# Cosine attention and token/channel mixer on one core: rows of a head laid out as three chunks of 128 and one of 64 instead of four of 112

## The chip, the cores and the metric

The kernel runs on one core of a Trainium2 chip. The metric is the device time of one execution in microseconds (us). Each version is executed several times; the median counts. Beside the times there is one profiled execution of the kernel, whose trace gives the durations used below.

## What is computed

The inputs are q, k and v with 8 batches, 12 heads, 448 rows and 64 features, in float32, and four weight matrices. The reference, cut to what matters:

```python
q_n = q / (norm(q, axis=-1) + 1e-06)
k_n = k / (norm(k, axis=-1) + 1e-06)
scores = q_n @ k_n.T / tau                  # per batch and head, 448 x 448
attn = softmax(scores)
x = (attn @ v), heads side by side          # 8 x 448 x 768
h = relu(x.T @ w_tok1) @ w_tok2             # 448 -> 256 -> 448, along the rows
u = x + h.T
out = u + relu(u @ w_ch1) @ w_ch2           # 768 -> 1536 -> 768, along the features
```

Row order inside a batch is free within the kernel, as long as q's rows, the output rows and the two token weights agree on it. Both versions use this freedom: they read several neighbouring rows of a head into one partition, and write the output rows back to where they belong.

## The kernel before

**Attention.** Two heads make a pair; there are 48 pairs, six per batch. `load` (line 151) brings q, k and v of a pair with one DMA each on the queue of SyncE (SP): partition p gets rows 4p to 4p+3 of a head, a run of 1 KB, so that a head lies as four chunks of 112 rows on 112 partitions. `squares` (line 164) squares q and k on GpSimd, `norm_sum` (177) adds up over the 64 features on VectorE, `norm_root` (181, 182) takes the root on ScalarE as exp(0.5 ln), `norm_rec` adds epsilon (186) and takes the reciprocal (188) on VectorE, and `normalize` (196) multiplies on GpSimd, four instructions of 256 elements per partition. The two heads are then transposed together to 128 features by 448 rows, in the first eleven pairs on TensorE (`tpose_pe`, 222, with a copy out of PSUM, 227 or 229), later by a DMA transpose on SP (`tpose_dma`, 213). `score` (241) computes the transposed scores: for each of four chunks of keys, two matmuls, one for each head. Head 0 uses rows 0 to 63 of the array, head 1 rows 64 to 127. `expo` (248) takes the exponential of a chunk, both heads in one ScalarE instruction of 896 elements per partition. `pv` (262) multiplies with v, which has a column of ones for the sum of the softmax: for each of four blocks of 128 query rows, 2 heads x 4 chunks = 8 matmuls with 65 columns; blocks 0 to 2 are the first half (24 matmuls), block 3 the second (8). Lines 268 and 269 divide.

**Mixer.** For each batch, `tok1` (293) and `tok2` (306, and 311 for the rows that two batches share in one tile) apply the token weights; the sum u goes to float32 and float16, and its float16 form is transposed by DMAs on SP (319 for batch 0, 327 later) into uT. `ch1` (335) needs all of uT of the batch; `ch2` (344) and the addition (348) follow, then `store` (363). A batch has three tiles of 128 rows, its odd neighbour four, the fourth of which holds the last 64 rows of both.

**Order of the work.** The order on every engine is written out by hand and kept by the program. For pairs 0 to 9 (`opening`) the mixer has little or nothing to give to TensorE; from pair 10 (`slot`) the mixer of the batch before is cut into jobs, and `fill` puts some of them between the attention steps, by costs and a credit per slot. Loads run four pairs ahead: `load(i + 4)` stands at the head of slot i in SP's queue, and after it there come, in this order of issue, the DMA transposes of uT, the transposes of normalized q and k of pair i + 2, and the stores. SP works through its queue in order, so an entry that waits holds up all behind it. Weights come with casting DMAs on GpSimd's queue (131, 136) and with plain ones on SP (110, 113, 114, 119); ScalarE casts the token weights to float16 in slots 3 to 5 (122, 125), w2 with a change of its column order.

**The tile of the array.** A matmul names a tile of TensorE's array. In the built program `pv`, `ch1`, `ch2`, `tok1` and most of `tok2` use the full 128 x 128, `score` uses 64 x 128 (64 rows, 128 columns) at rows 0 and 64, and line 311 uses 128 x 64 at columns 0 and 64.

## Time and profile before

| | |
|---|---|
| median of 3 runs | 417.53 us (416.78 to 418.73) |
| profiled execution | 414.94 us, of which its span is 413.2 us and 1.7 us lie around it |
| granted TensorE clock, mean | 0.991 |
| busy, share of the span | TensorE 94%, ScalarE 64%, VectorE 54%, GpSimd 53% |
| first ch1 matmul | at 62.5 us |
| last score matmul | at 351.6 us; then soon only the mixer of the last batch |
| DMA | 64.31 MB in 100249 packets, 96816 of them from the queues of SP and ScalarE |

"Span" is from the first to the last instruction; positions in the text are microseconds from its start. PE is TensorE's matmul row and PEld its weight loads, DVE is VectorE, ACT ScalarE, POOL GpSimd, SP (SPq) SyncE's queue. A row of a group of instructions names the line, the engine, the operation and the tiles (out<-in) with shapes as partitions x elements, a count, the busy time and the mean duration of one. Matmuls overlap in the pipeline, so that their mean duration is longer than their distance from start to start; where a matmul's cost matters, the distance is used.

### The profile page before, as it was taken

Reading aid. Unit: us, or ns where it says so; the run is one execution under the profiler, and the core shown is the slowest. Engines: PE = TensorE matmul, PEld = TensorE weight load, DVE = VectorE, ACT = ScalarE, POOL = GpSimd, SP = SyncE. Lnnn points to the kernel's source line nnn. Section 1 sums busy time; section 2 is a strip of 40 time slices with the busy share of each in tenths; the row PEclk is TensorE's granted clock in tenths of the full one; section 3 lists DMA queues with packets and bytes.
Section 4 is the critical chain, followed back from the end, with each engine's and each line's share of the span. In section 5 each row is a group of like instructions: output and inputs, shape, how many; then the busy total and the mean of one; then the engine's idle time right before and its main releaser. Section 6 shows DMA issues by size and latency. Waiting matters only on the chain.

```text
span 413.2 us, 8942 instructions
## 1 busy us (share of the span) xinstructions
PE 386.9 (94%) x3512; PEld 219.8 (53%) x3512; DVE 222.8 (54%) x520; ACT 263.0 (64%) x457; POOL 217.6 (53%) x307
## 2 busy tenths in 40 slices
PE   1787759999999999999999999999999999999996
PEld 1454535555545556555545556555545556655453
DVE  4786966649634575438643575448643573152022
ACT  5879767975587566766578566766578565521410
POOL 5999968856675465636675465636674440000000
PEclk9998998999999999999999999999999999999999
DMA  7999899876984478736865488738976453015013
GB/s 228 229 269 245 161 171 256 147 203 144 216 191 124 123 189 224 179 90 157 218 176 145 115 173 229 176 90 122 226 208 157 79 120 98 2 40 152 2 38 114
DMA packets 100249, 64.31 MB, mean 156 GB/s; under 512 B 60400, under 2 KB 96752, under 8 KB 100208
## 3 DMA queue, kind: packets, MB, share of 16 engines
q1 hardware_dynamic: 96816, 58.89, 58.2%
q0 software_dynamic: 3264, 4.72, 7.3%
q8 instruction: 27, 0.44, 0.4%
q10 hardware_dynamic: 128, 0.15, 0.1%
q14 instruction: 14, 0.11, 0.1%
HBM read 43.45 MB, written 11.01 MB: 132 GB/s over the span
## 4 chain that ended last, share of the span: by engine, by line
PE 82%; DVE 9%; ACT 5%; DMA 2%; issue 1%; POOL 0%; POOLq 0%; ACTq 0%
PE pG L335 27%; PE pF L344 26%; PE pO L262 10%; PE pS L241 10%; PE pR L293 5%; PE pU L306 3%; DVE u L316 3%; ACT pE L248 2%; DVE ssq L177 2%; DMA uT<-u 2%; DVE x L269 1%; DVE nre L186 1%; PE pU L311 1%; DVE u L324 1%; DMA ql<-in_q_dram 1%
## 5 line engine op out<-in xcount | busy, mean ns | idle before, releaser
L248 ACT ACTIVATE pE<-pS 112x896 f16<-112x896 f32 x192 | 165.7, 913 | 40.2 <-PE pS L241 39.3
L335 PE MATMUL pG<-uT,wc1t 128*128 128x384 f16 (+1 forms) x576 | 121.7, 354 | 0.2 <-DMA uT<-u 0.2
L196 POOL TENSOR_TENSOR qkn<-ql,rn 112x256 f16<-112x256 f32 x96 | 58.4, 627 | 112.6 <-DVE rn L188 103.1
L344 PE MATMUL pF<-wc2t,gT 128*128 128x384 f16 x672 | 116.4, 326 | 0.0
L344 PEld LDWEIGHTS <-gT 128*128 128x128 f16 x672 | 63.6, 98 | 47.1 <-issue 7.4
L337 ACT ACTIVATE gT<-pG 128x384 f16<-128x384 f32 (+1 forms) x96 | 52.6, 548 | 47.3 <-PE pG L335 46.6
L335 PEld LDWEIGHTS <-wc1t 128*128 128x128 f16 x576 | 51.2, 98 | 51.7 <-issue 11.8
L241 PE MATMUL pS<-qkT 64*112 64x448 f16 x384 | 63.0, 393 | 13.2 <-ACT pE L248 7.2
L348 DVE TENSOR_TENSOR u<-pF,u 128x384 f32<-128x384 f32 x56 | 31.1, 556 | 80.7 <-PE pF L344 80.7
L262 PEld LDWEIGHTS <-pE 112*128 112x128 f16 x1536 | 62.9, 100 | 18.0 <-issue 6.8
L262 PE MATMUL pO<-v,pE 112*128 112x65 f16 x1536 | 67.6, 197 | 0.1
L268 DVE RECIPROCAL rec<-pO 128x6 f32<-128x6 f32 x96 | 17.5, 183 | 85.5 <-PE pO L262 84.6
L177 DVE TENSOR_REDUCE ssq<-sq 112x16 f32<-112x1024 f32 (+1 forms) x49 | 58.5, 1194 | 5.9 <-ACT sq L162 4.2
L196 POOL TENSOR_TENSOR qkn<-kl,rn 112x256 f16<-112x256 f32 x95 | 57.3, 621 | 0.0
L164 POOL TENSOR_TENSOR sq<-ql 112x512 f32<-112x512 f32 x46 | 48.5, 1055 | 7.4 <-DMA ql<-in_q_dram 7.4
L164 POOL TENSOR_TENSOR sq<-kl 112x512 f32<-112x512 f32 x46 | 47.9, 1041 | 2.3 <-DMA kl<-in_k_dram 2.1
L269 DVE TENSOR_TENSOR x<-pO,rec 128x384 f16<-128x384 f32 x96 | 40.8, 425 | 3.3
L241 PEld LDWEIGHTS <-qkT 64*112 64x112 f16 x384 | 20.0, 129 | 40.3 <-issue 29.5
L316 DVE TENSOR_TENSOR u<-pU,x 128x384 f32<-128x384 f32 (+1 forms) x62 | 31.6, 547 | 2.0 <-PE pU L306 1.8
L326 ACT CAST u<-u 128x768 f16<-128x768 f32 x14 | 11.6, 832 | 21.6 <-DVE u L316 21.6
L293 PE MATMUL pR<-x,w1t 128*128 128x384 f16 x128 | 24.5, 333 | 0.3 <-DVE x L269 0.3
L306 PE MATMUL pU<-r,w2t 128*128 128x384 f16 x96 | 20.5, 328 | 1.2 <-DVE x L269 0.7
(34 smaller groups left out, 155.9 us busy)
## 6 DMA issues: line engine op xcount, KB each, us to landing
ql<-in_q_dram SPq DMA_DIRECT2D x48, 224.0 KB, 3.7
kl<-in_k_dram SPq DMA_DIRECT2D x48, 224.0 KB, 3.8
vl<-in_v_dram SPq DMA_DIRECT2D x48, 224.0 KB, 4.4
out_dram<-u SPq DMA_DIRECT2D x8, 336.0 KB, 3.4
wc1t<-in_moe_w_ch_dram POOLq DMA_DIRECT2D x6, 384.0 KB, 7.4
wc2t<-in_moe_w_ch_dram POOLq DMA_DIRECT2D x6, 384.0 KB, 5.2
out_dram<-u SPq DMA_DIRECT2D x8, 288.0 KB, 3.5
out_dram<-u SPq DMA_DIRECT2D x7, 240.0 KB, 3.1
```

What stands on the lines that cost most here:

```text
L164: nc.gpsimd.tensor_mul(out=s["sq"][:, j], in0=a, in1=a)
L177: nc.vector.tensor_reduce(out=small(i, "ssq")[:, j], in_=st_[i]["sq"][:, j], axis=AXX.X, op=ALU.add)
L196: eng.tensor_tensor(out=t[:, j, :, g, :], in0=s[nm][:, g], in1=_bcast_free(small(i, "rn")[:, j, NCH * g:NCH * g + NCH], E), op=ALU.mult)
L241: nc.tensor.matmul(pS[:, h, 0:S], s["T"][64 * h:64 * h + 64, 1, c * P:(c + 1) * P], s["T"][64 * h:64 * h + 64, 0, :], start=True, stop=True)
L248: nc.scalar.activation(out=s["p"][:, c], in_=s["pS"][c][:, :, 0:S], func=AF.Exp, scale=inv_tau)
L262: nc.tensor.matmul(pO[:, n, h, :], s["p"][:, c, h, c0:c0 + 128], s["v16"][:, NCH * h + c, 0:E + 1], start=(c == 0), stop=(c == NCH - 1))
L269: nc.vector.tensor_tensor(out=xt[hp:hp + nr, t0:t0 + len(ts), d0:d0 + 2 * E].rearrange("p t (h e) -> p t h e", h=2), in0=pO[m0:128, :, :, ...
L293: nc.tensor.matmul(pR[:], w1t[:, wi, tt * 128:(tt + 1) * 128], xt[:, xi, dh * DH:(dh + 1) * DH], start=(n == 0), stop=(n == 3))
L316: nc.vector.tensor_tensor(out=o[:, i - t0, cols], in0=pU[:], in1=xt[:, i, cols], op=ALU.add)
L335: nc.tensor.matmul(pG[:], wc1t[:, dt, ct * 128:(ct + 1) * 128], uT[:, dt, :], start=(dt == 0), stop=(dt == DT - 1))
L337: nc.scalar.activation(out=gT[:, ct, :], in_=pG[:], func=AF.Relu)
L344: nc.tensor.matmul(pF[:], gT[:, ct, (i - t0) * 128:(i - t0 + 1) * 128], wc2t[:, ct, dh * DH:(dh + 1) * DH], start=(ct == 0), stop=(ct == C ...
```

## The change

The 448 rows of a head are numbered 7m + r, with m from 0 to 63 and r from 0 to 6. Partition m of the lower half (0 to 63) and partition 64 + m of the upper half share the seven rows of m.

- **q and k in one tile** of seven slots of 128 partitions for each head: q in slots 0 to 2 and in the lower half of slot 3, k in the upper half of slot 3 and in slots 4 to 6. Squares, sums, roots and normalization run over this tile: 896 elements per partition for a pair instead of 1024, and normalization in two instructions of 448 instead of four of 256. The transposes take seven blocks of 128 instead of eight of 112.
- **v** keeps eight slots for a pair, with half slots for each head filled with zeros once at the start; there are five fixed v tiles in place of a pool of four.
- **Loads**: two DMAs each for q and k and four for v, in runs of 1 KB (four rows) and 768 bytes (three rows), on 64 partitions each: eight for a pair instead of three. For the first pair k goes through ScalarE's queue.
- **Scores**: three chunks of 128 keys and one of 64. In the last one both heads share a PSUM bank, head 0 in partitions 0 to 63, head 1 in 64 to 127; these two matmuls use tiles of 64 x 64 at (0, 0) and (64, 64). The exponential of this chunk covers 448 elements per partition for both heads.
- **pv**: the half chunk of both heads is one matmul with 130 columns against v padded with zeros; then six matmuls of 65 columns: seven for a block instead of eight.
- **Epsilon** is added by a sum over pairs: the root is written beside a constant 1e-6 that is set once, and a reduction adds the two.
- Token weights, output rows and the cast of w2 follow the new order of rows: w1 comes with two DMAs instead of eight, the cast of w2 takes six instructions instead of two, and all stores have 64 rows.
- At the start the load of ScalarE's table stands behind the first DMAs, and VectorE sets constants and zeros with 13 small instructions.

The diff, cut to its core:

```diff
-    P = 112
-    NCH = S // P
+    P, M, NCH, R = 128, 64, 3, 7
+    F3 = NCH * P
...
-    nc.scalar.add_instruction(mybir.InstLoadActFuncSet(
-        name=nc.get_next_instruction_name(), act_func_set_id=ACT_SET_LN_EXP,
-        ins=[], outs=[]))
...
-    v16s = [cst.tile([P, 2 * NCH, EV], FP16, name=f"v16_{n}") for n in range(4)]
+    vls = [cst.tile([P, 2 * NCH + 2, E], FP32, name=f"vl_{n}") for n in range(5)]
+    v16s = [cst.tile([P, 2 * NCH + 2, EV], FP16, name=f"v16_{n}") for n in range(4)]
+    nns = [cst.tile([P, 2, R, 2], FP32, name=f"nn_{n}") for n in range(3)]
...
+            nc.gpsimd.memset(t[M:P, NCH, E:E + 1], 0.0)
+            nc.gpsimd.memset(t[0:M, NCH + 1, E:E + 1], 0.0)
...
+    def zeros():
+        for t in nns:
+            nc.vector.memset(t[:].rearrange("p g r z -> p (g r z)"), EPS_NORM)
+        for t in vls:
+            nc.vector.memset(t[M:P, NCH, :], 0.0)
+            nc.vector.memset(t[0:M, NCH + 1, :], 0.0)
...
+    def w1_load():
...
+        rows = moe_w_tok1.rearrange("(m r) t -> m (r t)", r=R)
+        nc.sync.dma_start(out=st[0:M, 1:5, :].rearrange("p n t -> p (n t)"), in_=rows[:, 0:4 * T])
+        nc.sync.dma_start(out=st[M:P, 0:4, :].rearrange("p n t -> p (n t)"),
+                          in_=rows[:, 3 * T:7 * T])
...
-        nc.scalar.copy(out=w2t[:, tt, :].rearrange("k (c p) -> k c p", c=NCH),
-                       in_=stage["w2"][:, tt, :].rearrange("k (p c) -> k c p", c=NCH))
+        a = stage["w2"][:, tt, :].rearrange("k (m r) -> k m r", r=R)
+        for h in range(2):
+            nc.scalar.copy(
+                out=w2t[:, tt, 0:F3].rearrange("k (c h m) -> k h c m", c=NCH, h=2)[:, h],
+                in_=a[:, :, 4 * h:4 * h + NCH].rearrange("k m c -> k c m"))
+        nc.scalar.copy(out=w2t[:, tt, F3:S], in_=a[:, :, 3])
...
+        a = {n: x[b, 2 * pj:2 * pj + 2].rearrange("g (m r) e -> m g (r e)", r=R)
+             for n, x in (("q", q), ("k", k), ("v", v))}
...
+        if "qk" not in s:
+            s["qk"] = ld.tile([P, 2, R, E], FP32, name="qkl", tag="qkl")
+            s["v"] = vls[i % 5]
+        t = s["qk"][:].rearrange("p g r e -> p g (r e)")
...
+        parts = {"q": [(t[0:M, :, 0:E4], a["q"][:, :, 0:E4]),
+                       (t[M:P, :, 0:E3], a["q"][:, :, E4:E7])],
+                 "k": [(t[M:P, :, E3:E7], a["k"][:, :, E3:E7]),
+                       (t[0:M, :, E4:E7], a["k"][:, :, 0:E3])],
+                 "v": [(u[0:M, 0:E4], a["v"][:, 0, 0:E4]),
+                       (u[M:P, 0:E3], a["v"][:, 0, E4:E7]),
+                       (u[M:P, E4:E8], a["v"][:, 1, E3:E7]),
+                       (u[0:M, E8 - E3:E8], a["v"][:, 1, 0:E3])]}
         for nm in names:
-            t = ld.tile([P, 2, NCH, E], FP32, name=f"{nm}l", tag=f"{nm}l")
-            nc.sync.dma_start(
-                out=t[:].rearrange("p g c e -> p g (c e)"),
-                in_=src[nm][b, 2 * pj:2 * pj + 2].rearrange("g (p c) e -> p g (c e)", c=NCH))
-            st_[i][nm] = t
...
-                nc.scalar.activation(out=s["sq"][:, j], in_=a, func=AF.Square)
+            for o, x in parts[nm]:
+                (nc.scalar if i == 0 and nm == "k" else nc.sync).dma_start(out=o, in_=x)
...
+        s = st_[i]
+        s["sq"] = att.tile([P, 2, R, E], FP32, name="sq", tag="sq", bufs=2)
+        for z in range(2):
+            o, a = s["sq"], s["qk"]
+            if act:
+                nc.scalar.activation(out=o[:, :, PARTS[z]], in_=a[:, :, PARTS[z]], func=AF.Square)
             else:
-                nc.gpsimd.tensor_mul(out=s["sq"][:, j], in0=a, in1=a)
+                nc.gpsimd.tensor_mul(out=o[:, z], in0=a[:, z], in1=a[:, z])
...
+    def norm_sum(i, r=ALL):
+        nc.vector.tensor_reduce(out=small(i, "ssq")[:, :, r], in_=st_[i]["sq"][:, :, r],
...
+    def norm_root(i, r=ALL):
+        nc.scalar.activation(out=small(i, "ln")[:, :, r], in_=small(i, "ssq")[:, :, r], func=AF.Ln)
+        nc.scalar.activation(out=nns[i % 3][:, :, r, 0], in_=small(i, "ln")[:, :, r], func=AF.Exp,
+                             scale=0.5)
...
+    def norm_rec(i, r=ALL):
+
+        nc.vector.tensor_reduce(out=small(i, "nre")[:, :, r], in_=nns[i % 3][:, :, r, :],
+                                axis=AXX.X, op=ALU.add)
+        nc.vector.reciprocal(out=small(i, "rn")[:, :, r], in_=small(i, "nre")[:, :, r])
...
-    def norm_sum(i, j=BOTH):
-        nc.vector.tensor_reduce(out=small(i, "ssq")[:, j], in_=st_[i]["sq"][:, j], axis=AXX.X,
...
-    def norm_rec(i, j=BOTH):
-        nc.vector.tensor_scalar_add(out=small(i, "nre")[:, j], in0=small(i, "nrm")[:, j],
-                                    scalar1=EPS_NORM)
...
+        t = att.tile([P, R, 2, E], FP16, name="qkn", tag="qkn")
+        for z, r in enumerate(PARTS if first else (ALL,)):
+            for g in range(2):
+                eng = nc.vector if first and z and g else nc.gpsimd
+                eng.tensor_tensor(out=t[:, r, g, :], in0=s["qk"][:, g, r],
+                                  in1=_bcast_free(small(i, "rn")[:, g, r], E), op=ALU.mult)
...
+        for rs in (PARTS if first else (ALL,)):
+            pt = ps.tile([128, R, P], FP16, name="pT", tag="ps")
+            for r in range(rs.start, rs.stop):
+                nc.tensor.transpose(pt[:, r, :], s["qkn"][:, r].rearrange("p g e -> p (g e)"),
+                                    id16[:])
+            if first:
...
-            s["p"] = att.tile([P, NCH, 2, S], FP16, name="pE", tag="pE")
+            s["p"] = att.tile([P, R, S], FP16, name="pE", tag="pE")
...
+        kq = s["T"][:].rearrange("d r p -> d (r p)")
         for c in (2 * g, 2 * g + 1):
             pS = pss.tile([P, 2, 512], FP32, name="pS", tag="pS")
             for h in range(2):
-                nc.tensor.matmul(pS[:, h, 0:S],
-                                 s["T"][64 * h:64 * h + 64, 1, c * P:(c + 1) * P],
-                                 s["T"][64 * h:64 * h + 64, 0, :], start=True, stop=True)
+                d = slice(64 * h, 64 * h + 64)
+                if c < NCH:
+                    nc.tensor.matmul(pS[:, h, 0:S], kq[d, S + M + c * P:S + M + (c + 1) * P],
+                                     kq[d, 0:S], start=True, stop=True)
+                else:
+                    nc.tensor.matmul(pS[d, 0, 0:S], kq[d, S:S + M], kq[d, 0:S],
+                                     start=True, stop=True)
...
     def expo(i, c):
         s = st_[i]
-        nc.scalar.activation(out=s["p"][:, c], in_=s["pS"][c][:, :, 0:S], func=AF.Exp,
-                             scale=inv_tau)
+        if c < NCH:
+            o, a = s["p"][:, 2 * c:2 * c + 2], s["pS"][c][:, :, 0:S]
+        else:
+            o, a = s["p"][:, 2 * NCH], s["pS"][c][:, 0, 0:S]
+        nc.scalar.activation(out=o, in_=a, func=AF.Exp, scale=inv_tau)
...
+            nc.tensor.matmul(pO[:, n, :, :], s["p"][:, 2 * NCH, c0:c0 + 128],
+                             s["v16"][:, NCH:NCH + 2, 0:E + 1], start=True, stop=False)
             for h in range(2):
                 for c in range(NCH):
-                    nc.tensor.matmul(pO[:, n, h, :], s["p"][:, c, h, c0:c0 + 128],
-                                     s["v16"][:, NCH * h + c, 0:E + 1],
-                                     start=(c == 0), stop=(c == NCH - 1))
+                    nc.tensor.matmul(pO[:, n, h, :], s["p"][:, 2 * c + h, c0:c0 + 128],
+                                     s["v16"][:, (NCH + 2) * h + c, 0:E + 1],
+                                     start=False, stop=(h == 1 and c == NCH - 1))
...
-                ks = [(4 * e + t, t) for t in range(3)] + [(3, 3 + e)]
+                ks = [(4 * e + t, 1 + t) for t in range(3)] + [(3, 0 if e else 4)]
...
+                parts = [(h, 64 * h, 3) for h in range(2)]
             else:
-                f0 = 128 * (i % 4)
-                parts = [(e, f - f0, f, n) for f, n in f_segments(f0, f0 + 128)]
-            for z, (h, m, f, n) in enumerate(parts):
-                rows = out[2 * g + h].rearrange("(p c) d -> c p d", c=NCH)
+                parts = [(e, 64 * h, 4 * h + i % 4) for h in range(2)]
+            for z, (h, m, r) in enumerate(parts):
+                rows = out[2 * g + h].rearrange("(m r) d -> r m d", r=R)
                 queue = nc.scalar if end and z else nc.sync
-                queue.dma_start(out=rows[f // P, f % P:f % P + n, cols],
-                                in_=u32[m:m + n, i - t0, cols])
+                queue.dma_start(out=rows[r, :, cols], in_=u32[m:m + 64, i - t0, cols])
...
     load(0, "qk")
+    nc.scalar.add_instruction(mybir.InstLoadActFuncSet(
+        name=nc.get_next_instruction_name(), act_func_set_id=ACT_SET_LN_EXP,
+        ins=[], outs=[]))
+    zeros()
     load(1, "qk")
     ident()
     load(0, "v")
     load(2)
     load(1, "v")
     load(3)
```

## The prediction

> **What bounds the kernel now.** I read the page's slices first, then busy times by stretch, then timelines. The page's three busiest engines, in tenths for 40 slices of 10.3 us:
>
> ```profile
> PE   1787759999999999999999999999999999999996
> ...
> ACT  5879767975587566766578566766578565521410
> POOL 5999968856675465636675465636674440000000
> ```
>
> TensorE is full from slice 7 on, and not before. The same by stretch (columns: stretch, then busy us of PE, PEld, DVE, ACT, POOL, then granted clock, DMA share, GB/s):
>
> ```profile
> 10.00:20.00 10.00, 7.98 (x64) 4.57 (x60) 7.26 (x11) 9.07 (x15) 9.58 (x14) 1.00 0.93 235
> ...
> 30.00:40.00 10.00, 7.08 (x87) 4.57 (x86) 7.27 (x14) 9.87 (x19) 9.96 (x15) 0.84 1.00 251
> ...
> 50.00:64.00 14.00, 9.44 (x107) 5.74 (x107) 10.10 (x23) 8.41 (x15) 9.40 (x14) 0.88 1.06 174
> 64.00:85.00 21.00, 21.00 (x239) 12.23 (x238) 12.61 (x32) 19.24 (x36) 17.63 (x24) 1.00 0.97 217
> 85.00:208.00 123.00, 122.54 (x1139) 68.97 (x1137) 72.63 (x176) 81.72 (x142) 72.74 (x100) 1.00 0.69 170
> ```
>
> From 64 us PE is busy 21.00 of 21 and 122.54 of 123: there only TensorE's own work, or a stall put into its queue, changes the end. It holds 39 pairs: the list of PE groups from 64 us on has 78 score groups, two for each pair. The opening before it is paced by POOL (9.96 of 10 from 30 to 40) and ACT (9.87). So the sum has an opening part and a TensorE part.
>
> **Opening: what gets shorter.** POOL's slot of 5.05 us (normalization starts at 21.09, 26.14, 31.18, 36.23) is four normalizations 0.57 apart, two squares 1.00 apart and 0.76 to issue a weight DMA. By elements, squares go to 0.87 to 0.9 and the two new normalizations, 1.75 times as long as one of now, to 0.9 to 1.0: a slot of about 4.45. In a VectorE and GpSimd timeline the addition of epsilon (L186) shows its own cost:
>
> ```profile
> 18.03 2.35 DVE L186 TENSOR_SCALAR nre<-nrm 112x16 f32<-112x16 f32 x1
> ...
> 18.33 1.03 POOL L164 TENSOR_TENSOR sq<-ql 112x512 f32<-112x512 f32 x1
> ...
> 19.32 1.03 POOL L164 TENSOR_TENSOR sq<-kl 112x512 f32<-112x512 f32 x1
> 20.30 0.76 POOL L131 DMA_DIRECT2D wc1t<-in_moe_w_ch_dram  x1
> 20.42 0.25 DVE L188 RECIPROCAL rn<-nre 112x16 f32<-112x16 f32 x1
> 20.59 0.56 DVE L229 COPY qkT<-pT 128x896 f16<-128x896 f16 x1
> ```
>
> It takes 2.35 us where it took 0.17 at 13.09; it, and its neighbours of 1.06, 0.82 and 1.22, end within 0.1 us of the end of GpSimd's squares. A reduction does not do this: L177 takes 1.22 us beside GpSimd's work and without it. So the new addition costs about 0.2. But normalization on POOL starts at 21.09, right after the DMA issue ends at 21.06: POOL did not wait for it. Only the copy of the transposes did, at 20.59 instead of some 19.3; in the next slots it starts within 0.4 us of the last transpose. So this saves 1.3 us once and little more.
>
> ACT's exponentials are 0.81 apart for 896 elements; 448 should take 0.44 (L337 takes 0.495 for 384 and 0.60 for 512: 0.83 ns an element and 0.18 fixed, 0.55, less the overlap of 0.1 seen now): -0.37 a pair. The w2 cast runs at 0.99 for 448 strided elements; with the same 0.18 fixed that is 1.8 ns an element, and four of 192 and two of 64 take 2.7 instead of 2.0: +0.7, in slot 5, which ACT fills. Below nothing is excluded (no element less is copied, four instructions more); above, a longer stride could double it.
>
> **Opening: what gets longer.** SP issues a load of 224 KB in 0.45 to 0.58, and the six pieces of w1 on L110, 16 to 112 KB, in 0.42 to 0.69: the price is by DMA, not by size. Eight loads for a pair take 3.9 us instead of 1.5. The second half of k of pair 3, now within the tenth to twelfth DMA, becomes SP's 26th DMA: 0.76 + 25 x 0.49 = 13.0, and landing 2.8 later (first q: issued 0.76, awaited till 3.52), at 15.8. POOL, through with normalization 1 at some 13.5, waits 2.3 for it. Then squares 1.8, DMA issue 0.85, normalization 1.9, transposes 0.5, copy 0.6: scores of pair 2 start at 21.4 (now 21.21). From there POOL gains: pair 3 at 25.9 (26.49), pair 4 at 30.3 (31.37). Slots 3 to 5 are ACT's: -1.1 and +0.7; slots 6 to 8 give 0.1 to 0.4 each. W2 becomes SP's 65th entry, issued at 0.76 + 64 x 0.49 = 32 instead of 25.1; with its landing time of now, 8.2, it is there at 40 and holds a cast that ACT reaches at some 38; with fewer loads in flight it lands sooner: +0.5. Opening: **-1.5 us**. Bounds: -6 (0.6 in ten slots, if half loads issue in 0.31, the shortest row) and +3 (late loads and w2 not made good). VectorE's 13 settings and POOL's eight more lie before 4.18 and 6.00, where these engines wait for the first squares.
>
> **TensorE: the scores.** A PE timeline in the full stretch (start, busy us):
>
> ```profile
> 201.70 0.42 PE L262 MATMUL pO<-v,pE 112*128 112x65 f16 x8
> 202.05 0.58 PE L241 MATMUL pS<-qkT 64*112 64x448 f16 x4
> 202.57 1.47 PE L335 MATMUL pG<-uT,wc1t 128*128 128x512 f16 x6
> 203.88 0.93 PE L262 MATMUL pO<-v,pE 112*128 112x65 f16 x24
> 204.64 1.46 PE L335 MATMUL pG<-uT,wc1t 128*128 128x512 f16 x6
> ```
>
> A narrower window has the last pO at 201.93 and the second pair of pS at 202.29. Between matmuls of the same tile the distance goes by columns: 0.217 for the 512 of pG, so 0.19 for 448 and 0.028 for 65, and little else: pO takes 0.76 for 24, 0.032 each. At a change of tile it isn't: 201.93 to 202.05 is 0.12 for 0.03 of columns; 202.29 to 202.57 is 0.28 for 0.19. That is 0.09 to enter and 0.09 to leave; the first pair also waits 0.05 for its weights (202.05 to 202.29, 0.24). L311, tiles of 128 x 64, has the same: 0.77 for 0.64, its pairs side by side in one bank. The change puts a pair of 64 x 64 behind a pair of 64 x 128: one more change, 0.09, and 0.03 (L311's first pair) for weights: +0.12 a pair, x 39 = **+4.6**. Nothing covers it: PE works in order, and behind it stand full-tile matmuls of the mixer. No row shows this change of tile. Bounds: -1.2 (no wait at all and narrower weights, 0.03 x 39) and +12 (the two halves also one after the other, 0.19 more). I take 4.6: the rows nearest to it, two kinds of tile both ways, agree within 0.01. Wider key weights, 128 columns for 112, add at most 0.007 to each of 78 groups: **+0.5**.
>
> The Trainium skill has a rule against this change: TensorEngine Tiling (Array Packing), Key Properties, says that changing the tiling mode, not just the tile, drains TensorE. By it the 4.6 stands; if only row splitting counted as mode it would be nothing. The same page, Gotcha 1: PSUM Pressure, says that different row tiles cannot use one PSUM bank at once, which the half chunk does; by that it would be 12.0. No row here has row tiles in one bank.
>
> **TensorE: pv.** Eight matmuls of 32 ns are 0.256; now six and one of 130 columns (0.055 and 0.004 over, as for 65) are 0.251: -0.006 at most, four blocks, 39 pairs: **-1.0**. Bounds 0 and -5 (130 columns at the price of 65).
>
> **TensorE: late uT.** `ch1` needs the batch's last DMA transpose, and SP is backed up there:
>
> ```profile
> 190.48 0.58 SPq L151 DMA_DIRECT2D ql<-in_q_dram  x1
> 191.11 0.45 SPq L151 DMA_DIRECT2D kl<-in_k_dram  x1
> 191.60 0.46 SPq L151 DMA_DIRECT2D vl<-in_v_dram  x1
> 192.16 1.22 SPq L327 DMA_TRANSPOSE uT<-u  x1
> ...
> 197.29 1.27 SPq L327 DMA_TRANSPOSE uT<-u  x1
> ```
>
> From 189.2 to 201 SP never rests more than 0.1. Five more issues at 0.48 push the last uT from 197.29 by 2.4; it landed 4.4 after its issue, at 201.7, and pG starts at 202.57: stall 1.5. In the next odd batch (291.26, landed 3.3 later, pG 295.01; its loads wait before) it is 1.6 by a delay of 2.0; the batch at 104.84 has 1.9 to spare, those at 153.85 and 246.79 2.5 and 3. Together with small losses: less than 3.1, as ACT and DVE deliver sooner: **+2.4**. Bounds 0 and 5. The wait list has 0.2 us for pG on uT now. DMA transposes of q and k have a slot (8 us) of slack, stores end as before.
>
> **Sum.** -1.5 + 4.6 + 0.5 - 1.0 + 2.4 = +5.0. The profiled execution, 414.94 (span 413.2), becomes 419.9. That execution lies 2.6 under the median of the runs, 417.53, and I add the same difference to the median: **422.5**, 1.2% slower. ACT, DVE and POOL get 5 to 12% less to do after 64 us; that is worth nothing there, since PE has no wait for them.
>
> **Rivals.**
> - *No drain between the two row-split tiles.* Then the scores add nothing: 422.5 - 4.6 = 417.9, no change. For it: both modes split rows the same way. Against: every change of tile in this trace costs 0.09. 0.20.
> - *The opening pays.* POOL paces it, and with loads in time ten slots at -0.6 give -6, with some lost to ACT -4.5; without the drain and with uT just in time: -4.5 + 0.5 - 1.0 = -5.0, 412.5. It decides if SP issues a half load in about 0.31, so that k of pair 3 lands before 13.5. Against: 0.45 to 0.5 in the first 6 us. 0.18.
> - *The two halves of the last chunk one after the other*: 0.19 x 39 = +7.4 more, 429.9. Against: L311 shares a bank without it. 0.12.
>
> The forecast keeps 0.50, with 418.5 to 426.5 as its own range. Range: 414.0 leaves out most of the second rival, 430.0 takes in the third. A difference under 0.5% (415.4 to 419.6) is about what the runs can't tell from none. Faster: the second rival and a bit, 0.20; same: most of the first and the low end of the forecast, 0.22; slower: 0.58.
>
> **What would show it.** In the new trace: the distance from the second to the third score pair's weights (0.33 if drained, 0.19 to 0.24 if not) and between its two halves (0.003 or 0.19); PE's wait for uT at the first pG of a batch; POOL's wait before squares of pair 3, and the start of the first pG against 62.5 (61 forecast). Wrong would be: a DMA issue that is shorter for 64 partitions, half chunks that follow without a gap, or an opening that moves by more than 4 us.

## The result, and the profile after

The changed kernel takes **465.98 us** (median; 465.43 to 467.58) against 417.15 us of the kernel before on the same chip (416.63 to 418.73): ratio 1.117, 95% interval 1.1128 to 1.1211. It is 48.8 us slower; 422.5 was forecast, with a range up to 430. The forecast was 5.0 us, a tenth of it. Its direction was right, but largely by luck: its largest term, +4.6, stood for TensorE's scores, and the loss came with the loads.

The page of the changed kernel, the same slices as before (its 40 slices are 11.6 us each):

```profile
PE   1454863769978999799989899789988999999996
...
ACT  5455963548536766267446665366546755541410
POOL 3565656556343644434434544344624542000000
```

TensorE is not full from slice 7 on any more, and no other engine is full in its place. By stretch (columns as in the prediction):

```profile
10.00:20.00 10.00, 4.45 (x28) 2.13 (x29) 2.94 (x7) 6.17 (x12) 3.61 (x4) 1.00 0.48 130
30.00:40.00 10.00, 5.23 (x59) 3.49 (x59) 6.52 (x16) 6.46 (x14) 7.23 (x9) 0.83 0.94 186
50.00:64.00 14.00, 10.93 (x119) 6.86 (x118) 9.74 (x23) 11.49 (x23) 10.26 (x12) 0.88 0.95 196
64.00:85.00 21.00, 9.50 (x93) 5.33 (x91) 9.76 (x23) 7.67 (x15) 8.73 (x10) 0.73 0.83 140
85.00:208.00 123.00, 110.02 (x962) 60.17 (x963) 62.14 (x153) 72.17 (x134) 58.95 (x63) 0.96 0.70 155
```

From 10 to 20 us POOL is busy 3.61 instead of 9.58, and from 85 to 208 PE has 110.02 of 123 instead of 122.54. No engine paces either stretch: all wait. For what, the page's chain of work says in its two lines, by engine and by line; ahead of them stands the first line of the chain of before:

```profile
PE 82%; DVE 9%; ACT 5%; DMA 2%; issue 1%; POOL 0%; POOLq 0%; ACTq 0%
```

```profile
PE 48%; SPq 20%; DMA 17%; DVE 4%; POOL 4%; ACT 4%; issue 3%; POOLq 0%; ACTq 0%; DVEq 0%
PE pF L362 17%; PE pG L353 14%; SPq L168 14%; DMA qkl<-in_k_dram 9%; PE pS L252 4%; PE pO L280 4%; DMA qkT<-qkn 4%; POOL sq L181 3%; PE pR L311 3%; DMA uT<-u 3%; PE pU L324 2%; ACT pE L265 2%; SPq L345 2%; SPq L224 2%; DVE ssq L189 2%
```

In the chain of before, PE had 82%, and SP's queue isn't named. Now SPq, the issuing of DMAs on SP, has 20%, most of it on the loads' line L168, and DMA, the time from issue to landing, has 17%. The list of waits names the first to suffer (us in all, times, longest), here its first line:

```profile
POOL sq L181 <- DMA qkl<-in_k_dram: 128.1, 35, 6.2
```

GpSimd's squares waited 9.5 us for loads before (7.4 for q, 2.1 for k). And SP's own timeline in the steady part (start, us, line, times):

```profile
203.10 1.18 SPq L380 DMA_DIRECT2D out_dram<-u  x2
204.39 1.30 SPq L224 DMA_TRANSPOSE qkT<-qkn  x1
205.74 1.36 SPq L168 DMA_DIRECT2D qkl<-in_q_dram  x2
207.14 1.26 SPq L168 DMA_DIRECT2D qkl<-in_k_dram  x2
208.44 2.97 SPq L168 DMA_DIRECT2D vl<-in_v_dram  x4
211.53 1.24 SPq L224 DMA_TRANSPOSE qkT<-qkn  x1
```

Each entry begins within 0.12 us of the end of the one ahead. Over the whole trace an issue of a load takes 0.60 to 0.63 us at the median and the next begins 0.04 later: 5.1 us for the eight of a pair (5.7 in the rows shown, where one v load took 1.04). With 1.3 for the transpose of q and k and some 1.6 per slot for uT and stores, a slot costs SP 8.0 us. Summed over the whole trace, SP issues for 367 us, before for 190.

TensorE's granted clock is lower as well, 0.960 on the mean against 0.991. Its busy time is 392.9 us; in run e5 below, with the same matmuls and a clock of 0.986, it is 382.4. No run changes the clock alone, but these 10.5 us are the most that it can have added to the matmuls.

Three figures from each trace say more than the total. "First pG" is the start of the first `ch1` matmul: the opening lies before it. "Slot" is the distance between the first score matmuls of pairs 14 and 44, divided by 30. "SP per slot" is the time that SP spent issuing in that stretch, divided likewise. One slow execution each of e11, e15 and e16, 1.5% or more above the fastest of its kernel, is left out of the medians.

| kernel | median us (95% interval of the ratio to before) | first pG | slot | SP per slot | SP in all |
|---|---|---|---|---|---|
| before | 417.15 | 62.5 | 7.75 | 4.24 | 190 |
| changed | 465.98 (1.1128 to 1.1211) | 75.6 | 8.59 | 7.91 | 367 |
| e3: before, epsilon by pairs | 415.84 (0.9948 to 1.0003) | 62.1 | 7.75 | 4.28 | 191 |
| e2: before, eight loads | 458.62 (1.0936 to 1.1046) | 78.8 | 8.33 | 7.52 | 352 |
| e6: before, five tiny DMAs more | 453.18 (1.0832 to 1.0912) | 75.0 | 8.19 | 7.33 | 338 |
| e9: before, eight loads cut at 96 | 432.47 (1.0339 to 1.0416) | 69.7 | 7.84 | 6.47 | 296 |
| e5: changed, three loads | 413.29 (0.9888 to 0.994) | 58.8 | 7.74 | 4.61 | 201 |
| e17: changed, three loads in the opening | 443.46 (1.0619 to 1.0679) | 59.1 | 8.59 | 7.88 | 324 |
| e14: changed, loads a pair earlier | 471.60 (1.1285 to 1.1376) | 80.5 | 8.57 | 7.79 | 366 |
| e10: changed, two v loads on GpSimd | 429.62 (1.0259 to 1.0334) | 67.0 | 7.94 | 6.79 | 308 |
| e13: changed, four v loads on GpSimd | 434.94 (1.0354 to 1.0459) | 71.9 | 7.83 | 5.55 | 249 |
| e1: changed, v loads on ScalarE | 490.13 (1.17 to 1.18) | 81.7 | 8.98 | 5.58 | 253 |
| e7: changed, six loads | 437.74 (1.047 to 1.0556) | 67.8 | 8.07 | 6.69 | 309 |
| e11: two pairs per load | 436.67 (1.0405 to 1.051) | 73.3 | 8.00 | 5.44 | 255 |
| e12: the same, v on GpSimd | 435.94 (1.0381 to 1.0467) | 73.5 | 7.85 | 4.30 | 204 |
| e15: two pairs per load from the start | 435.31 (1.0411 to 1.0505) | 70.3 | 8.07 | 5.26 | 246 |
| e16: the same, v on GpSimd | 431.90 (1.0328 to 1.0397) | 69.3 | 7.87 | 4.20 | 205 |

### The profile page after: what moved, and what is told of

Its sections match the earlier page's. It is cut to its first block, busy times and chain, and to the rows that moved or that the text cites. A ratio compares the mean times of both kernels' runs of the same rounds, so it can differ in the third digit from the quotient of the medians.

```text
span 465.8 us, 8811 instructions
## 1 busy us (share of the span) xinstructions
PE 392.9 (84%) x3309; PEld 217.9 (47%) x3309; DVE 219.0 (47%) x533; ACT 249.4 (54%) x461; POOL 187.5 (40%) x221
## 4 chain that ended last, share of the span: by engine, by line
PE 48%; SPq 20%; DMA 17%; DVE 4%; POOL 4%; ACT 4%; issue 3%; POOLq 0%; ACTq 0%; DVEq 0%
PE pF L362 17%; PE pG L353 14%; SPq L168 14%; DMA qkl<-in_k_dram 9%; PE pS L252 4%; PE pO L280 4%; DMA qkT<-qkn 4%; POOL sq L181 3%; PE pR L311 3%; DMA uT<-u 3%; PE pU L324 2%; ACT pE L265 2%; SPq L345 2%; SPq L224 2%; DVE ssq L189 2%
## 5 line engine op out<-in xcount | busy, mean ns | idle before, releaser
L265 ACT ACTIVATE pE<-pS 128x896 f16<-128x896 f32 x192 | 148.2, 820 | 62.8 <-PE pS L252 62.8
L181 POOL TENSOR_TENSOR sq<-qkl 128x448 f32<-128x448 f32 x92 | 85.9, 954 | 137.9 <-DMA qkl<-in_k_dram 128.1
L353 PE MATMUL pG<-uT,wc1t 128*128 128x384 f16 (+1 forms) x576 | 124.8, 361 | 14.9 <-DMA uT<-u 14.8
L209 POOL TENSOR_TENSOR qkn<-qkl,rn 128x448 f16<-128x448 f32 (+2 forms) x97 | 91.6, 965 | 65.8 <-DVE rn L201 55.3
L252 PE MATMUL pS<-qkT 64*128 64x448 f16 x288 | 48.5, 386 | 25.8 <-DMA qkT<-qkn 17.7
L189 DVE TENSOR_REDUCE ssq<-sq 128x14 f32<-128x896 f32 (+2 forms) x49 | 52.1, 1064 | 23.6 <-POOL sq L181 19.6
L280 PE MATMUL pO<-v,pE 128*128 128x65 f16 x1152 | 61.2, 199 | 0.0
L280 PEld LDWEIGHTS <-pE 128*128 128x128 f16 x1152 | 54.4, 102 | 6.1 <-issue 0.5
L276 PE MATMUL pO<-v,pE 128*128 128x130 f16 x192 | 43.9, 229 | 0.1
L252 PEld LDWEIGHTS <-qkT 64*128 64x128 f16 x288 | 11.1, 95 | 51.9 <-DMA qkT<-qkn 22.8
L255 PE MATMUL pS<-qkT 64*64 64x448 f16 x96 | 19.1, 391 | 15.4 <-ACT pE L265 15.4
L276 PEld LDWEIGHTS <-pE 128*128 128x128 f16 x192 | 19.4, 101 | 13.2 <-issue 7.5
```

The lines of the kernel that those rows point to most:

```text
L181: nc.gpsimd.tensor_mul(out=o[:, z], in0=a[:, z], in1=a[:, z])
L189: nc.vector.tensor_reduce(out=small(i, "ssq")[:, :, r], in_=st_[i]["sq"][:, :, r], axis=AXX.X, op=ALU.add)
L209: eng.tensor_tensor(out=t[:, r, g, :], in0=s["qk"][:, g, r], in1=_bcast_free(small(i, "rn")[:, g, r], E), op=ALU.mult)
L252: nc.tensor.matmul(pS[:, h, 0:S], kq[d, S + M + c * P:S + M + (c + 1) * P], kq[d, 0:S], start=True, stop=True)
L265: nc.scalar.activation(out=o, in_=a, func=AF.Exp, scale=inv_tau)
L276: nc.tensor.matmul(pO[:, n, :, :], s["p"][:, 2 * NCH, c0:c0 + 128], s["v16"][:, NCH:NCH + 2, 0:E + 1], start=True, stop=False)
```

## The experiments

**First theories.** A: issuing on SP's queue sets the pace. B: transfers into half of the partitions land late, however they are issued. C: it is the rest of the change (tiles of the scores, epsilon, layout).

**e2, before with eight loads** (C against A and B):

```diff
-            nc.sync.dma_start(
-                out=t[:].rearrange("p g c e -> p g (c e)"),
-                in_=src[nm][b, 2 * pj:2 * pj + 2].rearrange("g (p c) e -> p g (c e)", c=NCH))
+            o = t[:].rearrange("p g c e -> p g (c e)")
+            x = src[nm][b, 2 * pj:2 * pj + 2].rearrange("g (p c) e -> p g (c e)", c=NCH)
+            for p in (slice(0, 64), slice(64, P)):
+                for g in (slice(0, 1), slice(1, 2)) if nm == "v" else (slice(0, 2),):
+                    nc.sync.dma_start(out=o[p, g], in_=x[p, g])
```

> The kernel before with its three loads of a pair split into eight: q and k by partitions 0 to 63 and 64 to 111, v also by head. Layout, work on the engines and bytes are those of before. A: 24 to 48 us slower than before (441 to 465), with SyncE issuing for over 85% of the middle of the run. B: about the same as A, since the transfers are as small. C: 417 to 420, since nothing but the loads is changed.

458.62 us. The old kernel with nothing but its loads cut up loses 42 us. C falls as the main cause.

**e5, the changed kernel with three loads** of 128 partitions each (partition p gets rows 3p to 3p + 3), everything else kept:

```diff
+        def rows(x, n):
+            y = x[b, 2 * pj:2 * pj + 2]
+            return bass.AP(tensor=y.tensor, offset=y.offset,
+                           ap=[[3 * E, P], [S * E, 2], [1, n * E]])
+        parts = {"q": [(t[:, :, 0:E4], rows(q, 4))],
+                 "k": [(t[:, :, E4:E7], rows(k, 3))],
+                 "v": [(u.rearrange("p (g f) -> p g f", g=2), rows(v, 4))]}
```

> The changed kernel with one DMA each for q, k and v of a pair, into all 128 partitions: partition p reads four (k: three) neighbouring rows from row 3p on. These are not the rows that belong there, so the output is not the reference's; shapes of tiles, all other work and the bytes of q and k are those of the changed kernel, v has 14% more. A: SyncE issues 3 loads of 0.45 to 0.6 instead of 8, and the kernel shows what the layout alone is worth: 408 to 418. B: also recovered, as the transfers are whole again. C: 455 or more.

413.29 us, 0.9% under the kernel before. So all of the loss comes with the eight loads, and the rest of the change, with three loads of 128 partitions, gains. (The rows that it reads overlap; what that alone does to the transfers was not measured.) GpSimd's timeline in its opening:

```profile
17.16 1.81 POOL L180 TENSOR_TENSOR sq<-qkl 128x448 f32<-128x448 f32 x2
18.93 0.76 POOL L131 DMA_DIRECT2D wc1t<-in_moe_w_ch_dram  x1
19.71 1.84 POOL L208 TENSOR_TENSOR qkn<-qkl,rn 128x448 f16<-128x448 f32 x2
21.50 1.81 POOL L180 TENSOR_TENSOR sq<-qkl 128x448 f32<-128x448 f32 x2
```

No gap, and a slot of 21.50 - 17.16 = 4.34 us where the kernel before had 5.05.

**e3, before with epsilon by pairs** (`nre` by a reduction over the root and a constant, nothing else):

> The kernel before with only the epsilon changed: added by a reduction over pairs (root, 1e-6) instead of a scalar addition. The prediction expects 1.3 us once and little more: 415.5 to 417.5. If the stall of the scalar addition beside GpSimd's squares (2.35, 1.06, 0.82, 1.22 us) were on the path that sets the end, it would be 3 to 5 us faster: 412 to 414. The addition should take 0.17 to 0.2 us everywhere.

415.84 us: no difference that these runs can tell, as forecast. The addition takes 0.158 to 0.187 us in all 49 places, where it took up to 2.35.

**e1, the changed kernel with the v loads on ScalarE's queue:**

```diff
-                (nc.scalar if i == 0 and nm == "k" else nc.sync).dma_start(out=o, in_=x)
+                (nc.scalar if nm == "v" or (i == 0 and nm == "k") else nc.sync).dma_start(out=o, in_=x)
```

> The changed kernel with the four v loads of every pair issued from ScalarE's queue instead of SyncE's; nothing else differs, bytes and shapes of all transfers stay. Theory A (issue): SyncE's queue paces the changed kernel. Each of its DMAs with 64 partitions takes 0.60 us to issue and 0.04 to the next, eight loads, a transpose of 1.24 and the mixer's share of 1.6 make about 8 us for a slot that TensorE fills in 7.4, so that loads lose their lead. With four loads fewer SyncE needs 5.4 us, and the kernel comes down to 412 to 425. Theory B (transfer): transfers into 64 partitions, with runs of 768 bytes, land late whatever queue issues them: 455 or more. Theory C (the rest of the change: tiles of 64 x 64, the half chunk, padded v) also expects 455 or more.

490.13 us. That is not A's 412 to 425; it lies in the open range of B and C, but none of the three expected a kernel slower than the changed one. The list of waits and ScalarE's timeline:

```profile
ACT pE L265 <- DMA vl<-in_v_dram: 77.9, 22, 7.5
```

```profile
203.57 2.61 ACTq L168 DMA_DIRECT2D vl<-in_v_dram  x3
206.23 1.73 ACT L265 ACTIVATE pE<-pS 128x896 f16<-128x896 f32 x2 [3.99 <-DMA vl<-in_v_dram]
```

ScalarE issues in order with its own work: exponentials stand behind the loads, TensorE waits for the exponentials (46.7 us). ScalarE was idle for 46% of the changed kernel's span and was still no place for them. The loads moved from one queue in order to another, and that queue also carries ScalarE's work, so the run does not tell A from B.

**e6, before with five tiny DMAs more per pair** on SP; its own three loads untouched:

```diff
+        if "v" in names:
+            t = ld.tile([64, 5, 16], FP32, name="xl", tag="xl")
+            for n in range(5):
+                nc.sync.dma_start(out=t[:, n], in_=v[b, 2 * pj, 64 * n:64 * n + 64, 0:16])
```

> The kernel before with its own three loads per pair, and five more DMAs per pair behind them on SP's queue, each of 64 partitions and 64 bytes a partition from v into a tile that nothing reads; 1 MB of traffic in all, and no transfer of the kernel's own is changed. Theory A (the number of issues on SP's queue sets the pace; 48 x 5 x 0.62 = 149 us are added to the 190 us that SP issues in the kernel before, as much as in the run with the split loads): 440 to 462 us. Theory B (it is the half-height transfers of q, k and v that land late, whichever way they are issued): 415 to 421 us.

453.18 us, in A's range. The transfers that matter are those of before and land no later (3.4 to 3.8 us after their issue at the median, before 3.7 to 4.4); 1 MB is added, and 36.7 us are lost. SP's timeline:

```profile
205.57 0.58 SPq L151 DMA_DIRECT2D ql<-in_q_dram  x1
206.20 0.47 SPq L151 DMA_DIRECT2D kl<-in_k_dram  x1
206.77 0.39 SPq L151 DMA_DIRECT2D vl<-in_v_dram  x1
207.21 3.03 SPq L158 DMA_DIRECT2D xl<-in_v_dram  x5
210.35 1.24 SPq L217 DMA_TRANSPOSE qkT<-qkn  x1
```

A DMA of 64 partitions and 64 bytes each takes as long to issue (0.594 us at the median) as the changed kernel's v loads of 64 KB (0.595).

**e9, before with eight loads cut at partition 96** (`slice(0, 96), slice(96, P)` in e2's edit):

> The kernel before with eight loads per pair as in the run with the split loads, but cut at partition 96 instead of 64: pieces of 96 and of 16 partitions. In the trace of before, DMAs of 96 and 16 partitions issued in 0.41 to 0.45 us, those of 64 in 0.58. Theory A with the price going by the number of partitions: 8 x 0.45 = 3.6 us of issuing per pair, 293 us on SP in all, 0.70 of the span: 418 to 432 us. Theory A with one price per DMA, and theory B (more and smaller transfers, whatever their issue): 452 to 462 us, as with the cut at 64.

432.47 us, half a microsecond over the first range. Same number of DMAs, same bytes, 26 us less than e2. Its timeline:

```profile
203.84 1.07 SPq L155 DMA_DIRECT2D ql<-in_q_dram  x2
204.96 0.92 SPq L155 DMA_DIRECT2D kl<-in_k_dram  x2
205.92 1.82 SPq L155 DMA_DIRECT2D vl<-in_v_dram  x4
```

0.457 each on the mean instead of 0.595. So of e2's 42 us, 16 come with the number of DMAs and 26 with the cut at 64, whose pieces of 64 and 48 partitions cost more to issue. Sooner landing is not what helped: e9's pieces land 2.3 to 3.0 us after their issue at the median, e2's 2.0 to 2.9.

**e10, the changed kernel with two of the four v loads on GpSimd** (`nc.gpsimd` for the pieces of the second head):

> The changed kernel with the two v pieces of the second head of each pair issued by GpSimd instead of SyncE; shapes, sizes and number of the transfers are as in the changed kernel. SP loses 2 x 0.62 x 48 = 60 us of issuing (367 to 307, 0.72 of a span of 425); GpSimd's slot becomes 4.4 + 2 x 0.78 = 6.0 us, below the 7.3 us of a slot. Theory A: 415 to 432 us. Theory B (the transfers are what is late): 455 to 468 us.

429.62 us. The transfers are those of the changed kernel, only their issuing moved to another queue, and 36 of the 49 us are back. Together with e6 this shows A for most of the loss. The single transfers aren't late either: the changed kernel's loads land 2.2 to 3.0 us after their issue at the median, the larger ones of before after 3.7 to 4.4. In the opening some land later, which e15 and the section on the prediction take up.

**e13, all four v loads on GpSimd:**

> The changed kernel with all four v pieces of every pair issued by GpSimd, none joined: SP 367 - 192 x 0.61 = 250 us as in the run with two pairs per load; GpSimd's slot is 4.4 + 4 x 0.54 = 6.6 us of 7.2, and its squares and normalizes stand behind the loads. Theory A: 416 to 428 us, no better than the run with two of the four pieces on GpSimd (429.6) if GpSimd's queue now takes SP's place in the opening, where it was busy 35 of 41 us. Theory B: 455 us or more.

434.94 us, over the range that was expected, and worse than with two, as its last clause allowed. The slot is better (7.83 against 7.94), the opening worse (71.9 against 67.0). GpSimd's busy time by stretch, e10's first line and e13's first line, columns as above:

```profile
0.00:41.00 41.00, 19.73 (x189) 11.98 (x190) 19.61 (x57) 26.69 (x54) 35.49 (x67) 0.98 0.85 197
```

```profile
0.00:41.00 41.00, 18.29 (x156) 10.42 (x156) 17.69 (x53) 22.45 (x45) 39.64 (x78) 0.84 0.82 189
```

With 39.64 of 41 GpSimd is now the one that paces the opening.

**e7, six loads with the right rows**: keys and values in another order, three rows per partition over 128 partitions and 64 rows apart; three casts of v instead of one.

> The changed kernel with six loads per pair, in a layout that gives the right rows: q as in the changed kernel (two DMAs of 64 partitions); the keys and values in another order of rows, 384 rows as three per partition over all 128 partitions (one DMA each for k and v) and the last 64 rows as the half chunk (one DMA each, 256 B a row). Three casts of v instead of one. Issuing per pair on SP by the rows of the runs so far: 2 x 0.62 + 2 x 0.50 + 2 x 0.55 = 3.3 us instead of 5.1, 285 us in all, 0.69 of the span. Theory A: 411 to 420 us. Theory B (half-height transfers land late, and q and the half chunk still are such): 435 to 460 us.

437.74 us, far over the range. Two of its own numbers were wrong: every load cost about 0.60, the 128-partition ones as well (598 ns at the median for k, where the same k load took 475 in e5), so that SP issues 309 us and not 285; and with the three casts VectorE is busy 30.4 us of 41, where e5 has 23.1 (126 to 167 us); the casts are 11.1 of it, in e5 2.2.

**e11 and e12, two pairs per load** from pair 4 on, with three buffers of two pairs; in e12 v by GpSimd:

```diff
+        t = qk2[:, z:z + n].rearrange("p z g r e -> p (z g) (r e)")
...
-        if i + AHEAD < N:
-            load(i + AHEAD)
+        if i + AHEAD < N and i % 2 == 0:
+            load(i + AHEAD, n=2)
```

> The changed kernel with the loads of two pairs joined in one DMA each from pair 4 on: eight DMAs for two pairs, in runs of 1 KB and 768 bytes as before, all on SP; same bytes, same rows, same arithmetic; three buffers of two pairs instead of four and five of one. 22 x 8 = 176 issues go, 176 x 0.635 = 112 us of SP's 367, which leaves 255. Theory A (issuing on SP sets the pace), by the runs so far (SP 201 us: 413; 308: 430 to 438): 413 to 422 us. Theory B (half-height transfers are what is late): 455 us or more.

> As the run with two pairs per load, and the v loads from pair 4 on issued by GpSimd: 88 issues of 0.6 leave SP (255 to 202 us, as in the run with three loads) and cost GpSimd 88 x 0.54 = 48 us, 1.1 us per slot on 4.4 of 7.2. Theory A: 410 to 416 us, faster than the kernel before if the rest of the change is worth what the run with three loads gained. Theory B: 455 us or more.

436.67 and 435.94 us. SP's sums came as expected (255 and 204), the times did not: they are 15 and 20 us over their ranges. So SP's sum isn't all, and A as it stood is too simple. Left open: throughput of the queue or lead time of the loads, opening or steady part, and whether joined loads land late. The last four runs go after these.

**e14, loads five pairs ahead** instead of four (`AHEAD = 5`, one more buffer each; w1 and w2 are loaded one slot sooner, so that they keep their place among the loads):

> The changed kernel with every load issued one pair earlier (five pairs ahead instead of four, with one more buffer of q and k and of v); number, shape and queue of the DMAs are as in the changed kernel. If the queue's throughput is the limit (5.1 us of loads, 1.3 of transpose of q and k and about 1.6 of the mixer's DMAs are 8.0 us per slot, where TensorE needs 7.2), an earlier place in the queue gains nothing: 456 to 468 us. If the loads only stand too late in the queue for GpSimd's squares (lead time), the part after the first pG falls from 390 us to about 355, the opening stays at 75.6: 425 to 440 us.

471.60 us, 3.6 over its range: nothing gained in the steady part (slot 8.57 against 8.59), 5 us lost in the opening. From 126 to 331 us the wait of the squares is gone from the list; what GpSimd and TensorE wait for there:

```profile
POOL qkn L209 <- DVE rn L201: 110.8, 24, 7.6
...
PE pS L252 <- DMA qkT<-qkn: 7.0, 7, 2.1
PE pG L353 <- DMA uT<-u: 6.7, 3, 3.1
```

The loads come in time and the pace is the same: of the 14.3 us that TensorE is idle in this stretch, 13.7 go to the two waits for DMA transposes, which stand in the same queue. It is throughput: 8.0 us of issuing in a slot for which TensorE alone needs 7.75. The slot is 8.6 and not 8.0, as the queue also waits: in the changed kernel SP waits 18.6 us in 21 places for GpSimd before it can issue a transpose of q and k (L224).

**e17, three loads for the first twelve pairs only**, then eight:

> The changed kernel with three DMAs of 128 partitions for the first twelve pairs (the opening) and its own eight from pair 12 on. The rows of the first twelve pairs are not the right ones and the zero blocks of v are overwritten, so the output isn't the reference's. It parts the 49 us: if the opening's share is what the first pG shows (75.6 against 58.8), first pG at 58 to 62 us and the rest near 385 to 390 us: 443 to 453 us. If a late opening is made good later: 460 us or more. If the opening is most of it: below 435 us.

443.46 us: the opening is back at 59.1, the slot stays at 8.59, the rest takes 382.0. It parts the loss: from e5 to e17 the steady part costs 30.2 us, from e17 to the changed kernel the opening costs 22.5. A part of the latter shows only behind first pG: first pG is 16.5 us apart in the two traces, the first score of pair 14 25.1 (95.2 and 120.3).

**e15 and e16, two pairs per load from the first pair on, six pairs ahead**; in e16 v by GpSimd from pair 14 on:

> The changed kernel with the loads of two pairs joined in one DMA from the first pair on, and six pairs ahead instead of four (four buffers of two pairs): SP issues 367 - 192 x 0.635 = 245 us, and the opening's four pairs take 10 us of issuing instead of 20. With throughput and lead time as the two causes of what the runs with joined loads still lost: first pG at 60 to 66 us (before 62.5, three loads 58.8), the rest 353 to 358 us as with three loads, 414 to 424 us in all. If transfers into 64 partitions are late in themselves (they landed after 4 to 6 us when joined, DMA share 1.19 in the opening): 432 to 440 us as before.

> As the run with all loads joined, with v from pair 14 on issued by GpSimd (68 issues of 0.62 = 42 us in all, 1.2 us per slot on 4.4): SP 245 - 42 = 203 us. If SP's share of 0.59 still costs something in the steady part: 2 to 4 us faster than the run with all loads joined; if not, within 2 us of it.

435.31 us, where the expectation put transfers that are late in themselves, and 431.90, 3.4 less, in the 2 to 4 that were expected from SP's share. SP has time now (5.26 and 4.20 per slot), yet first pG is at 70.3 and 69.3, and the slots are longer than 7.75. Two observations speak for the transfers themselves. The first is the busy times of the first 41 us, e5 and then e15, the last two columns being DMA share and GB/s:

```profile
0.00:41.00 41.00, 23.38 (x252) 14.26 (x253) 25.18 (x69) 33.88 (x70) 34.98 (x59) 0.96 1.00 271
```

```profile
0.00:41.00 41.00, 19.19 (x194) 11.82 (x194) 20.52 (x56) 26.52 (x54) 28.68 (x52) 0.92 1.05 220
```

The DMA share is 1.00 and 1.05, but all transfers together move 271 GB/s with e5's loads into 128 partitions and 220 with e15's into 64. The second is the landing: joined loads of 96 to 256 KB land after 4.3 to 5.1 us in e15 (DMA list, median), e5's of 192 and 256 KB after 3.6 to 4.3; k's 192 KB take 5.1 in e15 and 3.8 in e5. (The changed kernel's 2.2 to 3.0 are for half the bytes.) That is B, as a second limit that shows once the first is lifted. No run changes the landing alone, and the mix of transfers in the two stretches isn't the same, so its share isn't settled: against e5, 10.5 to 11.5 us of first pG and 0.1 to 0.3 us of a slot in e15 and e16 are what the sum of SP's issuing does not explain.

No version with the right rows beats the kernel before; e5, which would, reads other rows.

## Why the prediction failed, point by point

**What bounds the kernel.** Right for the kernel before: POOL's opening, TensorE's slots. But the list had no line for SP's queue, which was at 4.24 of 7.75 us per slot and about to be doubled. The prediction did see SP without a rest from 189.2 to 201 us, and used it for one late uT only.

**The step that failed: "the price is by DMA, not by size. Eight loads for a pair take 3.9 us instead of 1.5."** They take 5.1. The price isn't by size (e6), but it isn't one price either: loads of 64 partitions take 0.60 to 0.63 at the median. The nearest rows were there. SP's timeline of the kernel before has L110's pieces of 112, 16, 96 and 32 partitions (first row), of 80 and 48 (second), and right behind them the two pieces of w1 with 64 partitions:

```profile
14.39 1.86 SPq L110 DMA_DIRECT2D w1s<-in_moe_w_tok_dram  x4
...
19.27 1.42 SPq L110 DMA_DIRECT2D w1s<-in_moe_w_tok_dram  x2
20.73 0.58 SPq L113 DMA_DIRECT2D w1s<-in_moe_w_tok_dram  x1
21.35 0.59 SPq L114 DMA_DIRECT2D w1s<-in_moe_w_tok_dram  x1
```

An average over the wrong shapes hid them. The number decides twice, since 3.9 fits under both bounds and 5.1 under neither.

In the opening, loads at 5.1 us for a pair are slower than POOL's slot of 4.34. Up to 22.06 us the chain of work that ended last consists of SP's issues alone; k of pair 3 landed at 19.96, not at 15.8, and scores of pair 2 began at 26.57 instead of 21.4, those of pair 3 at 34.99 instead of 25.9. From there on the chain also holds landings: k loads issued at 22.06, 35.58 and 62.07 landed 5.7, 7.1 and 7.4 us later, the last two in stretches with a DMA share of 0.94 and 0.95. (Single loads of the kernel before took up to 6.9 us too.) So issuing isn't all of the opening. The prediction had one wait of 2.3 us for a late k, and none behind it.

In the steady part 5.1 + 1.3 + 1.6 = 8.0 is over TensorE's 7.75.

**The form of the step failed too.** The prediction put SP's extra work down as a start delay, made good later, and as five late issues for one uT (+2.4). It never added up SP's slot. e9 shows what that costs at nearly the forecast price (0.457): first pG at 69.7 instead of 62.5, slots of 7.84, 432.47 us. So even at the forecast's own price the eight loads cost 16 us, not the few that it allowed: the price goes with 26 of e2's 42 us, the form of the step with the other 16. Most of the 16 is the opening: in the traces pair 14 begins 12.5 us later than before (105.5 and 93.0), and the slots add 0.09 each. So the start delay was not made good; whether issuing or landing holds e9's opening up was not parted.

**Late uT: +2.4.** The direction was right. PE's timeline at the first batch:

```profile
75.57 1.15 PE L353 MATMUL pG<-uT,wc1t 128*128 128x384 f16 x3
83.93 0.48 PE L353 MATMUL pG<-uT,wc1t 128*128 128x384 f16 x1 [7.21 <-DMA uT<-u]
```

The wait is 14.8 us in five places, the longest 7.2.

**Opening: -1.5.** The gain on POOL was right (a slot of 4.34 in e5 for a forecast of 4.45, and first pG at 58.8), and it needed loads that kept up. They didn't: first pG moved by +13.1, far over the 4 us that the prediction named as a sign of being wrong, and w2 was issued at 45.91 instead of 32. The rival "the opening pays" had the right mechanism and the right condition, at -5.0 us: with the loads made cheap by other means, e5 is 3.2 us under the kernel before, and its first pG 3.7 earlier.

**Epsilon: "saves 1.3 us once and little more".** Right: e3 shows no measurable gain, though the instruction became up to thirteen times shorter.

**Scores: +4.6 and +0.5.** The mechanism is there, the size was off. PE's timeline of the changed kernel:

```profile
105.16 0.36 PE L252 MATMUL pS<-qkT 64*128 64x448 f16 x2
105.45 0.38 PE L255 MATMUL pS<-qkT 64*64 64x448 f16 x2
105.76 1.15 PE L353 MATMUL pG<-uT,wc1t 128*128 128x384 f16 x6
```

From the full pair to the half pair it is 0.29 us, and 0.31 to leave, for 0.19 of columns: the change of tile costs about 0.1, as forecast from the other tiles; the group takes 0.60 where it took 0.52, while 0.12 more was forecast. The Trainium skill's TensorEngine Tiling (Array Packing), Key Properties, that a change of tiling mode drains TensorE, agrees with these rows. But the group of two full pairs became shorter (0.48 instead of 0.52), with weights of 128 columns loading in 95 ns on the mean instead of 129 for 112 columns (PEld rows, L252 and L241). The "+0.5" for wider weights had the wrong sign, and the net is about +0.05 a pair. The halves run side by side in one bank (0.004 us apart); the rule on PSUM banks cited in the prediction is not borne out here. **pv: -1.0** held: 130 columns at 0.060, 65 at 0.032 apart. In e5, with no load in the way, a slot takes 7.74 against 7.75: scores and pv together cost nothing that shows, where the sum had +4.1 for 39 pairs.

**The range** ended at 430 so as to take in the third rival, 429.9. Even all upper bounds together (+3, +12, +0.5, 0 and +5) end at 438. The terms of the opening and of uT both hung on the same price of 0.48 to 0.49, and this one number had a bound below (0.31) and none above.

## What to carry to other kernels

Sum the issuing queue like an engine, per slot: every DMA on it, transposes and stores too, times the issue time of that very shape, beside the slot of the engine that bounds now. Leave room: at 6.5 and 6.8 us of issuing the slots were already 0.09 and 0.19 us longer than before's 7.75 (e9, e10). Cutting a load into more DMAs cost issue time here whatever its bytes; moving issues to a computing engine moves the cost into that engine's order, which can be worse than the queue (e1). When a wait disappears and the time stays (e14), look for the shared queue behind it.

## What the runs showed of the hardware

- Issue time on SP did not go by bytes: 0.60 us at the median for 64 partitions with 64 bytes or 1 KB each (e6, changed kernel), 0.42 to 0.46 for most pieces of 96 and 16 (e9), about 1.24 for a DMA transpose. It isn't the shape's alone either: the same k load of 128 partitions took 0.475 us in e5 and 0.598 in e7, among loads of 64, and w1's pieces of 64 took 0.58 and 0.59 in the kernel before and 0.47 in e2; why is open. GpSimd issued the 64-partition pieces in 0.52 to 0.56.
- The Trainium skill's DMA: Bandwidth & Descriptors, Issuing engines are not separate DMA queues, calls the sequencer's time to initiate a DMA usually small relative to the DMA. Here SP issued for 367 of 465.8 us, 0.6 for each transfer of 2.2 to 3.0, and that set the pace of the steady part (e14).
- In the first 41 us, at a DMA share of 1.05 and 1.00, all transfers together moved 220 GB/s where the loads went into 64 partitions (e15) and 271 where they went into 128 (e5).
